# Clustered attention and two feed-forward blocks: float32 transposes and centroid products set behind single score and value products

## The chip, the cores and the metric

The kernel runs on one core of a Trainium2 chip. The metric is the device time of one execution in microseconds (us). Below, TensorE is PE in the rows (PEld are its weight loads), VectorE is DVE, ScalarE is ACT, GpSimd is POOL and SyncE, which issues the transfers, is SP.

## What is computed

For 2 batches of 8 heads, 768 tokens and 64 columns: attention in which a query sees only the keys of its own cluster, then two feed-forward blocks on the 1536 x 512 result.

```python
q_assign = argmax(q_n @ c_n.T)          # nearest of 16 centroids of the head, by cosine
k_assign = argmax(k_n @ c_n.T)
scores = where(q_assign == k_assign, q @ k.T / 8, -1e9)
attn = exp(scores - max); attn = attn / (sum(attn) + 1e-9)
x = (attn @ v) as [1536, 512]
x = softplus(x @ w_in) @ w_out                       # 512 -> 2048 -> 512
out = (silu(x @ w_gate) * (x @ w_val)) @ w_out2      # 512 -> 1536 -> 512
```

All of it is float32.

## The kernel before

A float32 number is split into two float32r parts, hi and lo, and a product is the sum of hi*hi, hi*lo and lo*hi. The attention goes over eight pairs of heads, twelve tiles of 128 queries to a pair, 96 tiles in all. The line numbers are those of the kernel before.

**A tile.** `sc` (L460) forms the scores of 128 queries against 768 keys, four products of 384 columns into a bank pair `sps`, and VectorE takes the negative row maximum `nm` (L474). One tile later, `ex` (L477) has ScalarE write exp of them to `p`. Two tiles later, `tr` (L488) transposes `p` on TensorE, six float32 transposes of 128 x 128 into two banks `tps`, three to a bank; each bank is emptied twice, by ScalarE as `th` (the hi part, L504) and by VectorE as `tl` (the lo part, L505). There are two such banks, so the first transpose of a tile needs the first `tl` of the tile before. `pv` (L507) adds six value products of 256 columns to `ops`, and every second tile ScalarE copies the sum to `xa`.

**A pair's preparation**, during the tiles of the pair before: `prep_x` (L332) transposes its queries and keys, four times three float32 transposes into the one bank `mps` of the pool `ps_m`, emptied by ScalarE to `xr`; `prep_split_rows` has GpSimd split `xr` and SyncE move the rows to the operands QT and KT; `prep_sims` (L385) forms the centroid products `sims`, twelve calls of 32 columns in float32 (each shows as two matmuls in the trace); `prep_arg` (L395) finds the one-hot of the largest in four steps, on VectorE but for a product with `wi` on GpSimd (L412); `prep_oht` (L425) transposes the one-hots `oh`, twice three float32r transposes, emptied by ScalarE to `OH`.

**A pair's end**, during the next pair: `rec` and `rec_rows` (L550, L557) bring the reciprocal row sums, by one transpose and two transfers through memory, to `R`; `fin` (L570) multiplies by it on GpSimd (`xu`), takes the hi part `XH` on ScalarE (L577) and the lo part `XL` on GpSimd.

**The order** is written by hand. `step(i)` emits, for tile i, scores, exp of i-1, transposes of i-2, then whatever the table of events has for the tile, then value products ("setvp", L683). The events are set by offsets from the pair's start (L652). Each engine runs its instructions in this order. The centroid products alone are spread: `between` holds them, and `tr` emits one behind each of its transposes. `pump(2)` after tiles 0 and 26 puts in the narrowing and splitting of a weight tile (five instructions on VectorE, L116 to L135).

Of the kernel before, what the change touches and what calls it, by code (L numbers as in the profile page):

```python
# [40 lines left out]
def kernel(  # L41
# [60 lines left out]
    def w_narrow(loaded):  # L102
        """float64 bits [p, a, f, 2] (low word, high word) -> float32 [p, a, f], in two steps

        For 2^-126 <= |x| < 2^128 the float32 exponent is the top bit and the low
        seven bits of the eleven; magnitudes below and above are brought to that
        range's ends first."""
# [37 lines left out]
    # units of the two feed-forward blocks; a unit's own tiles are split three units  # L145
    # ahead, the tile of the output product with the unit
# [14 lines left out]
    # the first tiles of the second block's values have room early on  # L161
# [23 lines left out]
    def split_tasks(batch):  # L185
        """two steps for each tile"""
# [21 lines left out]
    # work of the other engines that is emitted between parts of the products  # L208
    todo = collections.deque()

    def first_do(tasks):
        """before all others, but for the second step of a tile whose first was done"""
# [13 lines left out]
    # ================= attention =================  # L226
# [105 lines left out]
    def prep_x(pr, which, half):  # L332
        src = (qn_t, kn_t)[which][pr]
        if half == 0:
            xr_t[pr, which] = pre.tile([128, S], F32, tag=f"xr{which}", name="xr")
# [634 lines left out]
```

## Time and profile before

| | |
|---|---|
| median of 3 runs | 863.29 us (862.83 to 864.06) |
| span of the profiled execution, first to last instruction | 861.7 us |
| TensorE busy | 820.9 us, 95% |
| VectorE busy | 683.9 us, 79% |
| ScalarE busy | 397.6 us, 46% |
| GpSimd busy | 336.0 us, 39% |
| attention | to 266 us of the span, feed-forward blocks from there |

The profile gives one execution. Its own time is known by its span only; the median of the runs is 1.6 us above it. The busy shares are means over stages of different kinds: in the feed-forward blocks TensorE runs long products with the others far behind it, in the attention all four engines are near the end of their room, and what counts there is which of them a tile waits for.

### The profile page before, as it was taken

The page shows a single profiled execution, that of the slowest core. Times are in us where ns is not written, and L with a number is a line of the kernel's source. Part 1 is how long each engine was busy: PE and PEld are TensorE (multiplying, and loading weights), DVE is VectorE, ACT ScalarE, POOL GpSimd, SP SyncE. Part 2 cuts the span into 40 slices and gives each one's busy share as a digit, 9 for nine tenths or more (in the row PEclk, how much of TensorE's full clock was granted, in tenths as well). Part 3 has the DMA queues.
Part 4 walks back from the last instruction along what each step waited for, and adds up shares of the span by engine and source line. Part 5 has one row for each costly group of instructions (what it writes and reads, how often), then busy time and mean ns, then how long its engine had stood idle before and what let it go on. Part 6 is the DMA issues. An engine that isn't in the chain of part 4 may idle for free.

```text
span 861.7 us, 11737 instructions
## 1 busy us (share of the span) xinstructions
PE 820.9 (95%) x4366; PEld 697.5 (81%) x4366; DVE 683.9 (79%) x1016; ACT 397.6 (46%) x735; POOL 336.0 (39%) x229
## 2 busy tenths in 40 slices
PE   7999999999999999989898997799999999999998
PEld 6899999999898778768777786588888888888886
DVE  6888978988896778898888888849886868876464
ACT  4689889888893755433244433232212212120210
POOL 3636465555522545444244333424433312332110
PEclk9799999999999999999999999999999999999999
DMA  8975775575312132122221120202312221220003
GB/s 200 248 163 134 190 150 142 141 172 122 85 38 69 49 98 74 51 74 80 65 74 50 49 74 25 68 7 74 97 50 74 74 73 49 74 72 26 1 1 146
DMA packets 65336, 75.42 MB, mean 88 GB/s; under 512 B 28960, under 2 KB 51584, under 8 KB 65280
## 3 DMA queue, kind: packets, MB, share of 16 engines
q1 hardware_dynamic: 65280, 74.68, 32.3%
q8 instruction: 34, 0.56, 0.3%
q14 instruction: 22, 0.18, 0.1%
HBM read 48.27 MB, written 3.19 MB: 60 GB/s over the span
## 4 chain that ended last, share of the span: by engine, by line
PE 60%; DVE 25%; DMA 5%; issue 4%; ACT 4%; POOL 1%; SPq 0%; POOLq 0%; ACTq 0%; DVEq 0%
PE bank L731 28%; PE bank L913 11%; PE sps L466 5%; PE ops L515 5%; DVE m L116 5%; PE tps L498 5%; DVE acc L827 5%; DVE e L796 3%; PE bank L813 2%; DVE r L789 2%; DVE m L126 2%; DVE m L123 2%; DMA rd<-rt 2%; DMA R<-rd 2%; DVE whi L135 2%
## 5 line engine op out<-in xcount | busy, mean ns | idle before, releaser
L136 POOL TENSOR_TENSOR wlo<-m,whi 128x512 fp32r<-128x512 f32 x68 | 100.7, 1480 | 291.9 <-DVE whi L135 266.1
L116 DVE TENSOR_SCALAR m<-m 128x512 f32<-128x512 f32 x68 | 86.0, 1265 | 38.4 <-ACT m L115 38.4
L505 DVE TENSOR_TENSOR tl<-tps,th 128x384 fp32r<-128x384 f32 x192 | 98.8, 550 | 20.2 <-ACT th L504 19.6
L474 DVE TENSOR_REDUCE nm<-sps 128x1 f32<-128x768 f32 x96 | 91.3, 952 | 14.3 <-PE sps L466 11.4
L498 PE MATMUL tps<-id,p 128*128 128x128 f32 x576 | 95.3, 282 | 1.1 <-DVE tl L505 1.1
L504 ACT CAST th<-tps 128x384 fp32r<-128x384 f32 x192 | 84.6, 491 | 20.1 <-PE tps L498 17.1
L482 ACT ACTIVATE p<-sps,nm 128x768 f32<-128x768 f32 x96 | 88.1, 918 | 5.6 <-DVE nm L474 5.6
L466 PE MATMUL sps<-KT,QT 128*128 128x384 f32 x384 | 84.7, 343 | 5.6 <-ACT p L482 3.7
L731 PE MATMUL bank<-YH,whi 128*128 128x512 f32 x288 | 81.6, 391 | 2.5 <-DVE acc L827 2.5
L498 PEld LDWEIGHTS tps<-id,p 128*128 128x128 f32 x576 | 76.4, 153 | 8.4 <-DVE tl L505 5.1
L731 PE MATMUL bank<-YL,whi 128*128 128x512 f32 x288 | 81.6, 392 | 0.0
L731 PE MATMUL bank<-YH,wlo 128*128 128x512 f32 x288 | 81.6, 392 | 0.0
L769 ACT CAST gh<-e 128x1536 fp32r<-128x1536 f32 x16 | 23.7, 1481 | 122.8 <-DVE e L796 122.8
L515 PE MATMUL ops<-th,VV 128*128 128x256 f32 x288 | 79.7, 306 | 0.0
L813 PE MATMUL bank<-gh,whi 128*128 128x512 f32 x192 | 58.9, 407 | 17.3 <-DVE r L789 8.2
L115 ACT ACTIVATE m<-raw 128x512 f32<-128x512 f32 x68 | 44.5, 666 | 62.1 <-POOL wlo L136 62.0
L515 PE MATMUL ops<-tl,VV 128*128 128x256 f32 x288 | 71.9, 279 | 0.0
L770 POOL TENSOR_TENSOR gl<-e,gh 128x1536 fp32r<-128x1536 f32 x16 | 57.1, 3573 | 34.5 <-ACT gh L769 30.7
L466 PEld LDWEIGHTS sps<-KT,QT 128*128 128x128 f32 x384 | 63.4, 191 | 6.7 <-ACT p L482 4.4
L731 PEld LDWEIGHTS bank<-YH,whi 128*128 128x128 f32 x288 | 54.4, 189 | 14.3 <-issue 2.9
L731 PEld LDWEIGHTS bank<-YH,wlo 128*128 128x128 f32 x288 | 54.5, 189 | 11.4
L731 PEld LDWEIGHTS bank<-YL,whi 128*128 128x128 f32 x288 | 54.5, 189 | 11.3
(124 smaller groups left out, 1776.6 us busy)
## 6 DMA issues: line engine op xcount, KB each, us to landing
raw<-in_moe_w_out_dram SPq DMA_DIRECT2D x28, 512.0 KB, 3.3
raw<-in_moe_w_in_dram SPq DMA_DIRECT2D x16, 512.0 KB, 3.9
QT<-hi SPq DMA_DIRECT2D x32, 192.0 KB, 3.1
raw<-in_moe_w_val_dram SPq DMA_DIRECT2D x12, 512.0 KB, 4.0
raw<-in_moe_w_gate_dram SPq DMA_DIRECT2D x12, 512.0 KB, 3.5
KT<-hi SPq DMA_DIRECT2D x14, 384.0 KB, 5.8
qn<-in_q_dram SPq DMA_DIRECT2D x16, 192.0 KB, 5.7
kn<-in_k_dram SPq DMA_DIRECT2D x16, 192.0 KB, 4.2
```

What stands on the lines that cost most here:

```text
L116: nc.vector.tensor_scalar(out=m.bitcast(F32), in0=m.bitcast(F32), scalar1=F64_LEAST, scalar2=F64_MOST, op0=ALU.max, op1=ALU.min)
L136: nc.gpsimd.tensor_tensor(out=lo, in0=x, in1=_r(hi), op=ALU.subtract)
L466: nc.tensor.matmul(ps[:, c, 0:384], lhsT=Q[:, a, 128 * j:128 * j + 128], rhs=K[:, a, 384 * c:384 * c + 384], start=(a == 0), stop=(a == 1),)
L474: nc.vector.tensor_reduce(out=nm, in_=ps[:, :, 0:384], axis=AX.XY, op=ALU.max, negate=True)
L482: nc.scalar.activation(out=_h(p), in_=s_t.pop(i)[:, :, 0:384], func=AF.Exp, bias=nm_t.pop(i), accum_out=sm_t[pr][:, j:j + 1],)
L498: nc.tensor.transpose(ps[:, 128 * j:128 * j + 128], p[:, 128 * kb:128 * kb + 128], id32)
L504: nc.scalar.copy(th, pv)
L505: nc.vector.tensor_tensor(out=tl, in0=pv, in1=_r(th), op=ALU.subtract)
L515: nc.tensor.matmul(o[:, 0:CW], lhsT=VV_t[pr][:, hh, kb].rearrange("p a d -> p (a d)"), rhs=t[:, kb, :], start=(kb == 0 and lohi == 0), sto ...
L731: nc.tensor.matmul(banks[c], lhsT=wt[:, kk, :], rhs=xt[:, kk, 512 * c:512 * c + 512], start=(kk == 0 and wt is hi and xt is xh), stop=(kk ...
L813: nc.tensor.matmul(banks[NCH * d + c], lhsT=wt[:, 0, ds_], rhs=gt[:, 512 * c:512 * c + 512], start=(ff == 0 and n == 0), stop=(ff == 1 and ...
L913: nc.tensor.matmul(bk, lhsT=lhs[:, ts_], rhs=rhs[:, 0, :], start=(ff == 0 and n == 0), stop=(ff == 1 and n == 2),)
```

## The change

It touches the attention only. The transposes of a tile go to a queue `tq`, and a preparation's transposes, centroid products, one-hot transposes and the transpose of `rec_rows` to a queue `fill`. `slot` takes one item from them behind each single score product and each single value product: behind the first two scores only from `fill`, and there only items that open no new bank; behind the others from `tq` as long as it holds any, then from `fill`. One bank of `ps_m` may be opened in a tile. What is left of `tq` follows the value products. exp of the tile before is now emitted ahead of the scores, and the events behind all of these.

Four things change beside the order. A pair's preparation begins 17 tiles before the pair, not 14. The product with `wi` moves from GpSimd to VectorE, as a fifth step of `prep_arg`. The one-hots are float32, not float32r, so their transposes are too. `XH` of all pairs but the last is written by GpSimd, not ScalarE.

On TensorE, in a tile that carries centroid products of the next pair, there stands before (sps are scores, tps the transposes of p, sims the centroid products, ops the value products, each row a call):

```order
L466 MATMUL sps<-KT_101,QT_97 128x384 x4
L498 MATMUL tps<-id_67,p 128x128
L377 MATMUL sims<-C_176,xr 128x32
L498 MATMUL tps<-id_67,p 128x128
L377 MATMUL sims<-C_176,xr 128x32
```

and in such a tile now:

```order
L515 MATMUL sps<-KT_101,QT_97 128x384
L421 MATMUL sims<-C_176,xr 128x32
L515 MATMUL sps<-KT_101,QT_97 128x384
L421 MATMUL sims<-C_176,xr 128x32
L515 MATMUL sps<-KT_101,QT_97 128x384
L561 MATMUL tps<-id_67,p 128x128
L515 MATMUL sps<-KT_101,QT_97 128x384
L561 MATMUL tps<-id_67,p 128x128
L575 MATMUL ops<-th,VV 128x256
L561 MATMUL tps<-id_67,p 128x128
L575 MATMUL ops<-tl,VV 128x256
```

The first transpose of p now stands ahead of the fourth score, and a centroid product has products of the loop on both sides.

On VectorE, around the one-hots of a pair (mx, eq and oh are steps of them, rt the copy of `rec_rows`), there stands before:

```order
L401 TENSOR_REDUCE mx<-sims 128x24
L474 TENSOR_REDUCE nm<-sps 128x1
L505 TENSOR_TENSOR tl<-tps,th 128x3x128 x2
L407 TENSOR_TENSOR eq<-sims,mx 128x384
L474 TENSOR_REDUCE nm<-sps 128x1
L505 TENSOR_TENSOR tl<-tps,th 128x3x128 x2
L562 COPY rt<-mps 12x128
L474 TENSOR_REDUCE nm<-sps 128x1
L505 TENSOR_TENSOR tl<-tps,th 128x3x128 x2
L416 TENSOR_REDUCE mx_986<-eq 128x24
L474 TENSOR_REDUCE nm<-sps 128x1
```

and now:

```order
L442 TENSOR_REDUCE mx<-sims 128x24
L524 TENSOR_REDUCE nm<-sps 128x1
L546 TENSOR_TENSOR tl<-tps,th 128x3x128 x2
L448 TENSOR_TENSOR eq<-sims,mx 128x384
L524 TENSOR_REDUCE nm<-sps 128x1
L546 TENSOR_TENSOR tl<-tps,th 128x3x128 x2
L455 TENSOR_TENSOR eq<-eq,wi 128x384
L524 TENSOR_REDUCE nm<-sps 128x1
L546 TENSOR_TENSOR tl<-tps,th 128x3x128 x2
L623 COPY rt<-mps 12x128
L458 TENSOR_REDUCE mx_958<-eq 128x24
L465 TENSOR_TENSOR oh<-eq,mx_958 128x384
```

The step with wi has come in, and rt and the last two steps stand together between two tiles.

On ScalarE, where a new pair's first transposes are copied out (xr), there stands before:

```order
L504 CAST th<-tps 128x3x128 x2
L577 CAST XH<-xu 128x768
L343 ACTIVATE xr<-mps 128x384
L482 ACTIVATE p,sm<-sps,nm 128x768
L504 CAST th<-tps 128x3x128 x2
L343 ACTIVATE xr<-mps 128x384
```

and on GpSimd now, at the end of a pair:

```order
L639 TENSOR_TENSOR xu<-xu,R 128x768
L642 CAST XH<-xu 128x768
L646 TENSOR_TENSOR XL<-xu,XH 128x768
L394 CAST hi<-xr 128x768
L395 TENSOR_TENSOR lo<-xr,hi 128x768
```

XH has left the queue in which it stood ahead of xr, and stands on GpSimd between its neighbours.

The diff, cut to its core (dropped comments and moved lines are left out):

```diff
+    tq, fill = collections.deque(), collections.deque()
+    bank_left = [0]
+    def slot(early=False):
+        if tq and not early:
+            tq.popleft()()
+        elif fill:
+            opens, f = fill[0]
+            if opens and (early or not bank_left[0]):
+                return
+            bank_left[0] -= opens
+            fill.popleft()
+            f()
+    def opening(items):
+        return [(n == 0, f) for n, f in enumerate(items)]
...
+    def queue_x(pr, which, half):
+        fill.extend(opening(items_x(pr, which, half)))
+    def queue_sims(pr):
+        fill.extend(opening(items_sims(pr, 0) + items_sims(pr, 1)))
...
     def prep_arg(pr, step):
         if step == 0:
-            assert not between
+            while fill:
+                fill.popleft()[1]()
...
-            eng = nc.gpsimd if pr else nc.vector
-            eng.tensor_tensor(out=eq, in0=eq, in1=wi.unsqueeze(1).to_broadcast(full), op=ALU.mult)
+        elif step == 2:
+            nc.vector.tensor_tensor(out=eq, in0=eq, in1=wi.unsqueeze(1).to_broadcast(full), op=ALU.mult)
...
-                oh = oh_t[pr] = pre.tile(full, F32R, tag="oh", name="oh")
+                oh = oh_t[pr] = pre.tile(full, F32, tag="oh", name="oh")
...
     def sc(i):
         for a in range(2):
             for c in range(2):
                 nc.tensor.matmul(ps[:, c, 0:384], ...)
+                if (a, c) == (1, 1):
+                    nm = ...
+                slot(a == 0)
...
     def pv(c, part):
                 nc.tensor.matmul(o[:, 0:CW], ...)
+                slot()
...
         elif part == 1:
-            nc.scalar.copy(XH[:, m, cols], xu)
+            if eng is nc.gpsimd:
+                eng.tensor_copy(XH[:, m, cols], xu)
+            else:
+                nc.scalar.copy(XH[:, m, cols], xu)
...
-    REC = (1, 5, 8, 10, 11)
+    REC = (1, 4, 8, 9, 10)
...
-            o = L * pr - 14 if pr > 1 else 0
+                off = {'x': (0, 1, 2, 3), 's': 4, 'p0': 4, 'p1': 6, 'a': (7, 8, 9, 10, 10), 't': (10, 11), 'v': 10, 'lq': 4, 'lv': 13}
+                o = L * pr - 17
...
     def step(i):
+        bank_left[0] = 1
+        ex(i - 1)
+        queue_tr(i - 2)
+        sc(i)
+        pv(c, part)
+        while tq:
+            tq.popleft()()
+        for f, a in events.pop(i, []):
+            f(*a)
...
+    queue_sims(1)
     for i in range(N_IT + 1):
         step(i)
```

## Rows read from the trace of the kernel before

**Rows 1.** Busy time by stretch: us, then PE, PEld, DVE, ACT, POOL, PEclk, DMA, GB/s.

```profile
18.30:34.40 16.10, 13.19 (x68) 12.23 (x69) 11.83 (x18) 7.50 (x17) 8.93 (x8) 0.68 1.02 278
34.40:230.20 195.80, 192.18 (x1531) 182.96 (x1529) 168.12 (x285) 169.77 (x399) 105.08 (x85) 1.00 0.66 151
```

**Rows 2.** Timeline of a plain tile, all engines: start, us (merged), engine, line, operation.

```profile
236.82 0.86 PE L466 MATMUL sps<-KT,QT 128*128 128x384 f32 x4
...
237.52 0.82 PE L498 MATMUL tps<-id,p 128*128 128x128 f32 x6
...
237.72 0.96 DVE L474 TENSOR_REDUCE nm<-sps 128x1 f32<-128x768 f32 x1
...
238.60 1.01 DVE L505 TENSOR_TENSOR tl<-tps,th 128x384 fp32r<-128x384 f32 x2
...
238.88 0.51 PE L466 MATMUL sps<-KT,QT 128*128 128x384 f32 x2
```

**Rows 3.** Centroid products alone, ahead of the loop: ns min/median/max, first and last start.

```profile
L377 PE MATMUL sims<-C,xr x24: 195/276/277, 9.1 to 11.6; 128*128 128x32 f32 x24
```

**Rows 4.** Timeline of TensorE where the transpose of 12 columns follows the six.

```profile
63.98 0.82 PE L498 MATMUL tps<-id,p 128*128 128x128 f32 x6
64.63 0.28 PE L560 MATMUL mps<-id,r 128*12 128x128 f32 x1
```

**Rows 5.** Timeline of TensorE in a tile with centroid products between its transposes.

```profile
209.61 0.31 PE L498 MATMUL tps<-id,p 128*128 128x128 f32 x1
209.76 0.31 PE L377 MATMUL sims<-C,xr 128*128 128x32 f32 x2
209.90 0.31 PE L498 MATMUL tps<-id,p 128*128 128x128 f32 x1
```

**Rows 6.** Timeline of VectorE around a step of the one-hots.

```profile
217.97 1.02 DVE L505 TENSOR_TENSOR tl<-tps,th 128x384 fp32r<-128x384 f32 x2
218.91 0.54 DVE L416 TENSOR_REDUCE mx<-eq 128x24 f32<-128x384 f32 x1
219.37 0.95 DVE L474 TENSOR_REDUCE nm<-sps 128x1 f32<-128x768 f32 x1
```

**Rows 7.** Timeline of TensorE, the score products that begin a tile.

```profile
69.58 0.86 PE L466 MATMUL sps<-KT,QT 128*128 128x384 f32 x4
...
72.13 0.87 PE L466 MATMUL sps<-KT,QT 128*128 128x384 f32 x4
...
74.43 0.86 PE L466 MATMUL sps<-KT,QT 128*128 128x384 f32 x4
...
76.81 0.86 PE L466 MATMUL sps<-KT,QT 128*128 128x384 f32 x4
...
80.18 0.86 PE L466 MATMUL sps<-KT,QT 128*128 128x384 f32 x4
...
91.54 0.86 PE L466 MATMUL sps<-KT,QT 128*128 128x384 f32 x4
...
94.46 0.86 PE L466 MATMUL sps<-KT,QT 128*128 128x384 f32 x4
...
227.09 0.87 PE L466 MATMUL sps<-KT,QT 128*128 128x384 f32 x4
...
230.18 0.98 PE L466 MATMUL sps<-KT,QT 128*128 128x384 f32 x4 [0.87 <-ACT p L482]
```

**Rows 8.** Timeline of ScalarE and TensorE where XH stands ahead of xr.

```profile
77.81 0.83 ACT L577 CAST XH<-xu 128x768 fp32r<-128x768 f32 x1 [1.15 <-POOL xu L575]
...
79.09 0.55 PE L340 MATMUL mps<-id,qn 128*128 128x128 f32 x3 [0.76 <-ACT xr L343]
```

**Rows 9.** Timeline of VectorE with the weight tile, and with the copy rt.

```profile
88.72 0.43 DVE L116 TENSOR_SCALAR m<-m 128x512 f32<-128x512 f32 x1
...
91.44 0.95 DVE L474 TENSOR_REDUCE nm<-sps 128x1 f32<-128x768 f32 x1
...
97.75 0.27 DVE L562 COPY rt<-mps 12x128 f32<-12x128 f32 x1
```

More of the change, by code (lines that the diff above doesn't have):

```diff
@@ L330, in mbank, with do_all, items_x, item @@
         return pool.tile([128, 512], dt, tag=tag, name=name)
[L332 to L345 removed]
+    def do_all(items):
+        for item in items:
+            item()
+    def items_x(pr, which, half):
+        src = (qn_t, kn_t)[which][pr]
+        got = []
+        def item(j):
+            if j == 0:
+                if half == 0:
+                    xr_t[pr, which] = pre.tile([128, S], F32, tag=f"xr{which}", name="xr")
+                got.append(mbank())
+            ps, t = got[0], 3 * half + j
+            nc.tensor.transpose(ps[:, 128 * j:128 * j + 128], src[:, t].rearrange("p h d -> p (h d)"), id32)
+            if j == 2:
+                cols = slice(384 * half, 384 * half + 384)
+                xr = xr_t[pr, which]
+                if which == 0:
+                    nc.scalar.activation(out=xr[:, cols], in_=ps[:, 0:384], func=AF.Copy, scale=SCALE)
+                else:
+                    nc.scalar.copy(xr[:, cols], ps[:, 0:384])
+                x_done.add((pr, which, half))
+        return [functools.partial(item, j) for j in range(3)]
+    x_done = set()
+    def prep_x(pr, which, half):
+        do_all(items_x(pr, which, half))
+    def queue_x(pr, which, half):
+        fill.extend(opening(items_x(pr, which, half)))
     def prep_split(pr, which, eng, hilo=None):
+        assert {(pr, which, 0), (pr, which, 1)} <= x_done
         xr = xr_t[pr, which]
@@ L375, in sims_tile @@
     def sims_tile(pr, which, t):
+        if which == 0 and t == 0:
+            y_t[pr] = mbank(name="sims")
         y = y_t[pr]
@@ L383, in sims_tile, with items_sims @@
         )
-    def prep_sims(pr, which, spread=True):
-        if which == 0:
-            y_t[pr] = mbank(name="sims")
-        for t in range(NT):
-            if spread:
-                between.append(functools.partial(sims_tile, pr, which, t))
-            else:
-                sims_tile(pr, which, t)
+    def items_sims(pr, which):
+        return [functools.partial(sims_tile, pr, which, t) for t in range(NT)]
+    def queue_sims(pr):
+        fill.extend(opening(items_sims(pr, 0) + items_sims(pr, 1)))
     def prep_arg(pr, step):
@@ L486, in ex, with evac, queue_tr @@
         p_t[i] = p
-    def tr(i):
+    def evac(i, half, ps):
+        c, jj = divmod(i, CT)
+        th = th_t[c][:, 3 * half:3 * half + 3, 128 * jj:128 * jj + 128]
+        tl = tl_t[c][:, 3 * half:3 * half + 3, 128 * jj:128 * jj + 128]
+        pv = ps[:, 0:384].rearrange("p (a n) -> p a n", a=3)
+        nc.scalar.copy(th, pv)
+        nc.vector.tensor_tensor(out=tl, in0=pv, in1=_r(th), op=ALU.subtract)
+    def queue_tr(i):
         c, jj = divmod(i, CT)
@@ L493, in tr, with item @@
         p = p_t.pop(i)
-        for half in range(2):
-            ps = ps_t.tile([128, 512], F32, tag="t", name="tps")
-            for j in range(3):
-                kb = 3 * half + j
-                nc.tensor.transpose(ps[:, 128 * j:128 * j + 128], p[:, 128 * kb:128 * kb + 128], id32)
-                if between:
-                    between.popleft()()
-            th = th_t[c][:, 3 * half:3 * half + 3, 128 * jj:128 * jj + 128]
-            tl = tl_t[c][:, 3 * half:3 * half + 3, 128 * jj:128 * jj + 128]
-            pv = ps[:, 0:384].rearrange("p (a n) -> p a n", a=3)
-            nc.scalar.copy(th, pv)
-            nc.vector.tensor_tensor(out=tl, in0=pv, in1=_r(th), op=ALU.subtract)
+        banks = {}
+        def item(kb):
+            half, j = divmod(kb, 3)
+            if j == 0:
+                banks[half] = ps_t.tile([128, 512], F32, tag="t", name="tps")
+            ps = banks[half]
+            nc.tensor.transpose(ps[:, 128 * j:128 * j + 128], p[:, 128 * kb:128 * kb + 128], id32)
+            if j == 2:
+                evac(i, half, ps)
+        tq.extend(functools.partial(item, kb) for kb in range(NT))
     def pv(c, part):
@@ L568, in rec_rows, with queue_rec @@
         r_t[pr] = R
+    def queue_rec(pr):
+        fill.append((True, functools.partial(rec_rows, pr)))
     def fin(pr, part, eng, c0=0, c1=S):
@@ L615 @@
     mpool[0] = (ps_m, "m")
-    for n in range(4):
+    for n in range(5):
         prep_arg(0, n)
```

110 lines of the change are left out of this document (46 added, 64 removed).

## The prediction

> **What bounds the kernel now.** I read four views, in this order. The table by stretches says which engine fills the attention loop; the timeline of a plain tile says what a tile costs on each engine and who waits for whom; the rows of the other kinds of tile give the price of each extra; the starts of successive tiles show where TensorE waits. From 34.4 to 230.2 us TensorE is busy 192.2 of 195.8 us, VectorE 168.1, ScalarE 169.8, GpSimd 105.1 [rows 1]. So the loop is TensorE's, but not by much. A plain tile takes 2.06 us, from scores at 236.82 to scores at 238.88 [rows 2]: 0.70 for four score products, 0.65 for six transposes (the same six stand alone from 63.98 to 64.63 [rows 4]), 0.70 for six value products. VectorE works 1.82 of these: the row maximum nm holds it 0.88 (237.72 to 238.60 [rows 2]), the two subtractions tl 0.94 (217.97 to 218.91 [rows 6]). It is idle only 0.24 us in a plain tile. That nearness decides this forecast.
>
> The blocks behind 266.4 us are untouched, and I take their time as it is. The profiled span is 861.7 us and the median of the runs 863.29, 1.6 us more; the changes below are added to the median.
>
> **The change, step by step: what TensorE itself does.** The order of the 128x128 transposes is new, their number is not. A float32 transpose costs 0.11 us in a burst. Is that the load of its weights, which a longer product ahead could hide, or its own stream? In rows 4 the sixth transpose is followed by one with 12 weight columns only (mps<-id,r), and the six still take 0.65 us. A load of 12 columns cannot be what holds the sixth to 0.11, so it is the stream, and moving it behind a product gives nothing back. Nor does a change between the two kinds of product cost anything that I can see: 4 scores, 6 transposes and 6 value products fill the 2.06 us with two such changes, and no remainder over 0.01 us is left. The change makes ten more of them in a tile. The only excess I grant is that the weight load of the next product (0.11, below) just outlasts a transpose's stream: 0.002 us for five more in each of 94 tiles, **+1.0 us**, with -3 and +4 as bounds.
>
> The centroid products (sims) are another matter. Each is two short matmuls with a 128-column load each. Alone, 24 of them went out between 9.1 and 11.6 us [rows 3], 0.11 us each, far more than 32 columns can need: they run at the pace of their loads. Before, one call stood between two transposes: from 209.61 to 209.90 us, 0.29 for both [rows 5], so 0.18 for the call, since a transpose's own stream hides one load and the transpose's load is short (0.29 less two loads leaves 0.07). After, the call stands between two products of the loop. The product ahead hides its first load, but the second load and the load of the product behind lie open: 2 x 0.11 = 0.22. That is 0.04 dearer, for 12 calls in each of the six pairs prepared in the loop: 72 x 0.04 = **+2.9 us**. If loads could be drawn two ahead, the call would cost 0.14 and this term would be -2.9 instead; that is its other bound.
>
> The Trainium skill (TensorE: Matmul & The Clock Gate, LDWEIGHTS (loading the stationary operand)) puts a load at columns over 1.2, 107 ns for 128 columns, and lets it run under the matmul ahead. Rows 3 agree with it at 0.11. By that rule alone a call behind a product would take 0.214, the term would be +2.4 and the forecast 0.5 us lower; it speaks against this part of the change.
>
> The one-hot transposes (mps<-idr,oh) turn from float32r into float32. The second such tile took 74.43 - 72.13 = 2.30 us, 0.24 over plain for three [rows 7], 0.08 each; float32 ones cost 0.11. 42 x 0.03 = **+1.3 us**.
>
> **What goes away.** Before, the copy of XH stands in ScalarE's queue ahead of the copy that empties the bank of a new pair's first transposes. XH waited until 77.81 for GpSimd, and TensorE's next three transposes waited 0.76 for the bank, until 79.09 [rows 8]. That tile took 80.18 - 76.81 = 3.37 us against 2.39 for such a tile (2.06 and three transposes), and the last one of the kind, at 227.09, 3.09 against 2.06, its wait seen at 230.18 [rows 7]. Counted over five such places, with the tile behind each, 5.6 us. The change puts XH on GpSimd, whose queue has 195.8 - 105.1 = 90 us of room [rows 1], and starts the pair three tiles sooner, with an item or two behind each product: **-5.6 us** (or -4, if something else keeps the bank). The first one-hot tile took 2.55 against 2.30 for the second [rows 7]: TensorE waits there for the one-hots. After, the transposes stand at the end of the next tile: 6 x 0.25 = **-1.5 us**.
>
> **What comes new: VectorE.** This is the step I weigh most. Before, the first transpose of a tile stands 0.70 us behind the start of its scores (237.52 - 236.82), and nm starts at 0.90 (237.72) [rows 2]. The bank that this transpose fills is emptied by the first tl of the tile before, which ends at 0.90 + 0.88 + 0.55 = 2.33 (0.55 is the 1.02 of two in rows 6 less the 0.47 from one start to the next); it is wanted at 2.06 + 0.70 = 2.76. VectorE may run 0.43 us late. After, the transpose stands behind the third score, at 0.53, and itself puts the fourth score and so nm off by 0.11. The tl ends at 2.44 and is wanted at 2.59: 0.15 us of grace. One step of the one-hots holds VectorE 0.46 (218.91 to 219.37 [rows 6]), and before that was hidden but for 0.03: it stands there between tl and nm, which then starts late by as much [rows 6]. Now there are five steps, since the product with wi comes over from GpSimd; the first runs beside the last centroid products, four fall into tiles with almost nothing extra on TensorE, the last two into one, with the copy rt (0.27 [rows 9], 0.20 as the next begins before its end, which a one-hot step's 0.54 and 0.46 show too). Per pair: 4 x 0.46 + 0.20 = 2.04, less the grace 0.15, less two tiles' idle 0.48, less the four float32 transposes that TensorE does there, 0.44: 0.97 us in which TensorE waits. Six pairs: **+5.8 us**. The bounds are 0 (VectorE finds room) and 2.04 x 6 = 12.
>
> The weight tile that is split at tile 26 puts 2.72 us on VectorE (88.72 to 91.44 [rows 9]). Before, it stood between two long tiles, and cost the tile from 91.54 to 94.46 2.92 - 2.06 = 0.86 [rows 7], with the tile behind it 1.15. After, it stands behind the last centroid products and a one-hot step: the last of these products ends 0.28 us into the next tile (its length in rows 3), so nm can start at 0.28 + 0.46 + 2.72 = 3.46 instead of 1.01, 2.30 us late after the grace. 2.30 - 1.15: **+1.2 us**.
>
> **The start.** From 18.3 to 34.4 us the mean granted clock is 0.68 [rows 1], so TensorE has its lower level, 1.2 GHz, for some 10 of the 16 us (0.32 of the clock lost, at a half lost while it is low). The second pair's centroid products leave tiles 2 and 3 for tiles 0 to 2, where TensorE idled; it is fuller before the clock falls, which may shorten the slow stretch. Against that stand five one-hot steps in tiles 4 to 6, packed closer, 0.9 by the sum above, and 0.2 for a later first nm. I take **-0.6 us**: bounds -4 (no slow stretch, half of some 8 busy us) and +2.
>
> **The sum**: 1.0 + 2.9 + 1.3 - 5.6 - 1.5 + 5.8 + 1.2 - 0.6 = +4.5 us, 863.3 + 4.5 = **867.8 us**.
>
> **The rivals.** First, faster: VectorE never makes TensorE wait. Then the 5.8 is gone, and the weight tile costs nothing, not even its old 1.15: 867.8 - 5.8 - 1.2 - 1.2 = 859.6 us. For it: VectorE has 0.24 us idle in each tile [rows 2, 6] and took a one-hot step in its stride before. Against: that took a grace of 0.43, of which 0.15 is left. Second, no difference: half of these waits come, and the start gains 1 to 2 us, near 863.5. Third, much faster: a transpose behind a product costs 0.06 instead of 0.11, 0.05 x 6 x 94 = 28 us, near 840; rows 4 speak against it. Fourth, much slower: the first transpose is held by its semaphore so often that its load lies open too, 0.07 for each of some 500 places in an extreme, up to 35 us more; in plain tiles the grace is positive, so I give it little. The deciding point between the forecast and the first rival is whether tl of one tile ends 0.5 us behind the next tile's scores.
>
> **How the numbers follow.** Forecast, slower, 865 to 873: 0.51. First rival 0.22, third 0.03: faster 0.25. Second 0.22. Fourth 0.02 with the forecast: slower 0.53. The range takes in the first rival and the forecast with the larger half of the one-hot waits: 859 to 873; the 2 in 10 left out are the third and fourth and the outer ends of VectorE's term. A measurement of this kernel can tell about 0.2%, 1.7 us, from no change.
>
> **What would show it.** Right: a centroid call of 0.22 us; tiles of 2.06 us with transposes and products in turn; no wait of mps for xr; waits of tps for tl, 1 us in each pair, in the three tiles behind its last centroid products, and some 2 us at tile 27. Wrong: plain tiles shorter than 2.05 us (third rival), longer than 2.10 (the grace is already used up), or no waits for tl (first rival).

## The result and the profile after

| | before | after |
|---|---|---|
| median of four runs | 863.67 us (862.83 to 865.56) | 874.24 us (871.40 to 877.31) |
| span of the profiled execution | 861.7 us | 875.4 us |
| starts of the first score product, tile 12, tile 84, the last value product | 18.33, 50.11, 230.18, 266.04 us | 17.62, 52.72, 240.09, 277.30 us |

The ratio is 1.0123, with a 95% interval of 1.009 to 1.0156: slower by 1.2%, 10.6 us, where 4.5 us were forecast and 873 us was the upper end of the range. The direction was right, the size was not. The mean granted clock is not the cause: it was 0.982 to 0.990 (mean 0.986) in the four runs after and 0.986 on the mean over the 64 runs of the kernel before that stand beside it and the runs below. One of the four executions of the run burst2 below took 2087 us and is left out of its ratio.

By place, in the two profiled executions (tiles are counted from 0): 2.6 us were lost by tile 12, 7.3 in tiles 12 to 83 (187.4 against 180.1 us), 1.35 from tile 84 to the last value product, and 2.4 in the untouched blocks behind it, which had five stretches at the lower clock, of 3.4 us each, against three before. Such stretches come in another number in each execution (three to six in the traces below), so I take these 2.4 us as no part of the change.

The stretches of the kernel after, which answer to [rows 1] (the columns are those of [rows 1]; the third is the end of the attention):

```profile
17.60:33.70 16.10, 15.06 (x67) 14.00 (x68) 11.80 (x17) 7.36 (x16) 7.85 (x7) 0.58 1.00 272
33.70:240.10 206.40, 200.31 (x1533) 188.04 (x1532) 182.11 (x295) 171.09 (x395) 106.26 (x85) 1.00 0.63 144
240.10:277.40 37.30, 34.41 (x250) 31.78 (x249) 28.77 (x50) 27.31 (x63) 10.01 (x6) 1.00 0.13 36
```

TensorE is still 97% busy in the loop, now for 206.4 us instead of 195.8. The busy share doesn't show such a loss: in the centroid rows below the record of a score product lasts 0.42 us, though the next matmul starts 0.26 us behind it.

Two plain tiles, to set beside [rows 2] (start, us, engine, line, operation; the rows that the reading doesn't need are left out):

```profile
248.65 0.68 PE L515 MATMUL sps<-KT,QT 128*128 128x384 f32 x3
248.98 0.38 ACT L593 COPY xa<-ops 128x256 f32<-128x256 f32 x1
249.25 0.92 ACT L533 ACTIVATE p<-sps,nm 128x768 f32<-128x768 f32 x1
249.66 0.96 DVE L524 TENSOR_REDUCE nm<-sps 128x1 f32<-128x768 f32 x1
250.14 1.05 ACT L545 CAST th<-tps 128x384 fp32r<-128x384 f32 x2
250.66 1.12 DVE L546 TENSOR_TENSOR tl<-tps,th 128x384 fp32r<-128x384 f32 x2
250.74 0.69 PE L515 MATMUL sps<-KT,QT 128*128 128x384 f32 x3
251.27 0.14 PEld L561 LDWEIGHTS tps<-id,p 128*128 128x128 f32 x1 [0.16 <-DVE tl L546]
251.82 0.96 DVE L524 TENSOR_REDUCE nm<-sps 128x1 f32<-128x768 f32 x1
...
253.00 0.70 PE L515 MATMUL sps<-KT,QT 128*128 128x384 f32 x3
```

The tile from 248.65 to 250.74 took 2.09 us, the one behind it 2.26. (That one carries the transpose of 12 columns too; its like without it take 2.16.) In the second the first transpose waits for tl. But VectorE is hardly late: nm began at 249.66, and tl can follow it after 0.88 (as in [rows 2]), at 250.54. It begins at 250.66, since its th came only at 250.14, behind exp, which stands behind xa on ScalarE. In every second tile ScalarE has xa to copy, and there its chain takes most of the time. So the prediction's sign "longer than 2.10, the grace is already used up" came true, in half of the tiles and by an engine that it had not reckoned with.

A centroid call between two score products of the kernel after:

```profile
181.64 0.42 PE L515 MATMUL sps<-KT,QT 128*128 128x384 f32 x1
181.90 0.30 PE L421 MATMUL sims<-C,xr 128*128 128x32 f32 x2
182.03 0.42 PE L515 MATMUL sps<-KT,QT 128*128 128x384 f32 x1
```

From score to score it is 0.39 us; less the 0.175 of a score product alone, a call costs 0.22, as forecast.

To count the rest, I take each tile's length less what it carries, at the prices that the tiles without a wait and the spacing of starts give: before, 2.06 us for a plain tile and 0.11, 0.185 and 0.06 for a transpose of the preparation, a centroid call and a one-hot transpose; after, 2.084 and 0.1135, 0.2235 and 0.1125. (The 0.18 of [rows 5] is a call with a transpose behind it; the last of the six in a tile has a value product behind it, so a tile with six took 3.17, 0.185 a call.) What is left is called the wait of a tile below.

| tiles 12 to 83 | forecast, us | measured, us |
|---|---|---|
| order of transposes and products (72 x 0.025) | +0.8 | +1.8 |
| centroid calls (72 x 0.0385) | +2.9 | +2.8 |
| one-hot transposes and the wait for the one-hots | -0.4 | +1.9 |
| waits for xr gone (these tiles alone) | -5.1 | -5.1 |
| VectorE's waits | +5.8 | +4.2 |
| weight tile | +1.2 | +1.25 |
| five preparation transposes fewer in the stretch | | -0.3 |
| rests of 0.08 to 0.12 in nine tiles | | +0.8 |
| sum | +5.2 | +7.3 |

The worst line is the one-hots'. Their transposes, set a tile later so as not to wait, waited in all six pairs: 0.20, 0.20, 0.65, 0.43, 0.34 and 0.28 us, against 0.29 to 0.32 before. This is the wait in the start, at pair 1 (tile 6), where it was longest (VectorE, GpSimd and TensorE rows):

```profile
37.41 0.54 DVE L458 TENSOR_REDUCE mx<-eq 128x24 f32<-128x384 f32 x1
37.99 1.87 DVE L465 TENSOR_TENSOR oh<-eq,mx 128x384 f32<-128x384 f32 x1
39.79 0.94 DVE L524 TENSOR_REDUCE nm<-sps 128x1 f32<-128x768 f32 x1
...
37.63 1.82 POOL L395 TENSOR_TENSOR lo<-xr,hi 128x768 fp32r<-128x768 f32 x1 [0.21 <-DMA QT<-lo]
...
39.92 0.30 PE L477 MATMUL mps<-id,oh 128*64 128x128 f32 x1 [1.16 <-DVE oh L465]
```

The step oh takes 0.56 us elsewhere. Here it takes 1.87, and ends at 39.86, 0.41 us behind the end of GpSimd's lo at 39.45. In the seven pairs of this trace it took 0.56, 0.56, 0.63, 0.70, 0.78, 0.99 and 1.87 us, and each long one ended 0.41 to 0.42 us behind the end of a GpSimd instruction that was running when it began. That gave the theory for the second half of the experiments.

The theories at the start: **A**, the sum was right in kind, and the order on TensorE costs what it takes from VectorE's room; **B**, VectorE's extra work must be made good in whatever order.

### The profile page after: what moved, and what is told of

Its sections match the earlier page's. It is cut to its first block, busy times and chain, and to the rows that moved or that the text cites. A ratio compares the mean times of both kernels' runs of the same rounds, so it can differ in the third digit from the quotient of the medians.

```text
span 875.4 us, 11741 instructions
## 1 busy us (share of the span) xinstructions
PE 833.6 (95%) x4366; PEld 705.8 (81%) x4366; DVE 698.5 (80%) x1023; ACT 398.6 (46%) x728; POOL 336.2 (38%) x229
## 4 chain that ended last, share of the span: by engine, by line
PE 62%; DVE 29%; issue 4%; ACT 3%; DMA 1%; POOL 1%; SPq 0%; DVEq 0%; ACTq 0%
PE bank L793 27%; PE bank L975 11%; PE ops L575 6%; PE sps L515 6%; PE tps L561 6%; DVE m L116 5%; DVE acc L889 4%; PE bank L875 3%; DVE tl L546 3%; DVE nm L524 3%; DVE e L858 3%; DVE m L126 2%; DVE r L851 2%; DVE m L123 2%; DVE whi L135 1%
## 5 line engine op out<-in xcount | busy, mean ns | idle before, releaser
L561 PE MATMUL tps<-id,p 128*128 128x128 f32 x576 | 142.9, 278 | 3.8 <-DVE tl L546 3.4
L515 PE MATMUL sps<-KT,QT 128*128 128x384 f32 x384 | 117.4, 397 | 2.4 <-DMA KT<-khl 1.8
L546 DVE TENSOR_TENSOR tl<-tps,th 128x384 fp32r<-128x384 f32 x192 | 102.5, 553 | 11.0 <-ACT th L545 5.2
L545 ACT CAST th<-tps 128x384 fp32r<-128x384 f32 x192 | 91.5, 482 | 34.8 <-PE tps L561 32.8
L575 PE MATMUL ops<-th,VV 128*128 128x256 f32 x288 | 104.4, 363 | 1.4 <-DVE xu L597 1.4
L575 PE MATMUL ops<-tl,VV 128*128 128x256 f32 x288 | 102.1, 355 | 0.0
L561 PEld LDWEIGHTS tps<-id,p 128*128 128x128 f32 x576 | 81.1, 141 | 12.4 <-DVE tl L546 11.5
L515 PEld LDWEIGHTS sps<-KT,QT 128*128 128x128 f32 x384 | 69.6, 199 | 5.8 <-DVE KT L697 1.5
```

The costliest lines, as they stand in the source:

```text
L515: nc.tensor.matmul(ps[:, c, 0:384], lhsT=Q[:, a, 128 * j:128 * j + 128], rhs=K[:, a, 384 * c:384 * c + 384], start=(a == 0), stop=(a == 1),)
L545: nc.scalar.copy(th, pv)
L546: nc.vector.tensor_tensor(out=tl, in0=pv, in1=_r(th), op=ALU.subtract)
L561: nc.tensor.transpose(ps[:, 128 * j:128 * j + 128], p[:, 128 * kb:128 * kb + 128], id32)
L575: nc.tensor.matmul(o[:, 0:CW], lhsT=VV_t[pr][:, hh, kb].rearrange("p a d -> p (a d)"), rhs=t[:, kb, :], start=(kb == 0 and lohi == 0), sto ...
```

## The experiments

**XH alone.** The kernel before with the one edit that was to help:

```diff
-            nc.scalar.copy(XH[:, m, cols], xu)
+            if eng is nc.gpsimd:
+                eng.tensor_copy(XH[:, m, cols], xu)
+            else:
+                nc.scalar.copy(XH[:, m, cols], xu)
```

> The kernel before with one part of the change alone: XH of all pairs but the last is written by GpSimd, and nothing else moves. Theory (the term of -5.6 us in the prediction): the bank of a new pair's first transposes then comes free in time, the five waits of mps for xr (0.37 to 1.1 us in tiles 23, 35, 47, 71 and 83) and the 0.25 us behind each go away, and the last value product comes at 266.0 - 5.6 = 260.4 us, the median at about 858 us. Rival: the copy to xr is late for another reason (exp and the two th stand ahead of it too), XL comes later on GpSimd and holds something else: less than 2 us are gained, 862 to 864 us.

860.05 us, 0.9942 of the kernel before (0.9916 to 0.9968). Tiles 12 to 83 took 174.98 us, 5.1 less. Score products that begin a tile, ScalarE and GpSimd there, to set beside [rows 7] and [rows 8]:

```profile
77.17 0.86 PE L466 MATMUL sps<-KT,QT 128*128 128x384 f32 x4
78.53 0.49 PE L340 MATMUL mps<-id,qn 128*128 128x128 f32 x3
79.56 0.86 PE L466 MATMUL sps<-KT,QT 128*128 128x384 f32 x4
...
76.92 0.50 ACT L343 ACTIVATE xr<-mps 128x384 f32<-128x384 f32 x1
...
77.91 0.83 POOL L578 CAST XH<-xu 128x768 fp32r<-128x768 f32 x1
```

The tile that took 3.37 us takes 2.39. The prediction's largest gain is right, and it needs nothing of the new order: this version beats both kernels, the one before by 0.6%.

**The burst again.** First in a simple form, in which the places that the transposes left went to the other items:

```diff
-        if tq and not early:
-            tq.popleft()()
-        elif fill:
+        if fill:
...
             sc(i)
+        while tq:
+            tq.popleft()()
```

> The changed kernel with one part undone: the six transposes of a tile stand in one burst between its scores and its value products again; centroid products, the preparation's transposes and the rest stay behind single products. Theory A (the order on TensorE costs little by itself, but takes away VectorE's room): 0.025 us a tile come back (2.4 us), and with the first transpose back at 0.70 us behind the tile's start the waits of tps for tl, about 1.0 us in a pair, fall to some 0.3: 2.4 + 4 + 1 at the last tile = 7 us less, the last value product near 270 us instead of 277.3, median near 867. Theory B (VectorE's extra work has to be made good in any order): only the 2.4 us come back, last value product near 275 us, median near 872.

881.63 us, 1.0215 (1.019 to 1.0241), slower than the kernel after. It tells nothing of the burst: the one-hot transposes had moved up as well and waited 1.75 us a pair for the one-hots (10.5 us in six waits of mps for oh). So again, every other item held at its place:

```diff
-        if tq and not early:
-            tq.popleft()()
+        if skip[0] and not early:
+            skip[0] -= 1
...
+        skip[0] = len(tq)
             sc(i)
+        while tq:
+            tq.popleft()()
```

> The changed kernel with the six transposes of a tile in one burst between scores and value products, and every other item at exactly the place that it has in the changed kernel (in the run burst the one-hot transposes had moved up as well, and waited 1.75 us a pair for the one-hots). Theory A (the order takes away VectorE's room): 0.025 us a tile come back (2.4 us), tiles 84 to 94 are 2.06 us, and the waits of tps for tl in the one-hot tiles (about 0.33 + 0.38 us a pair) fall below 0.2 a pair; with 1 us at the last tile some 6 us less, last value product near 271 us with a start like that of the changed kernel. Theory B (VectorE's extra work has to be made good in any order): these waits stay, last value product near 274 us.

869.52 us, 1.0072 (1.0051 to 1.0094), 4.7 less than the kernel after. Tiles 84 to 94 are 2.06 us again but for two, and the end from tile 84 takes 35.3 us instead of 37.2; tiles 12 to 83 take 185.6 instead of 187.4. The wait of 0.33 us two tiles behind the last centroid products is gone (0.00). So the order took this room, as A says. The 0.38 in the tile behind VectorE's double step stays (0.35), as B says: there VectorE is later than any grace. And the wait for the one-hots grew from 2.1 to 3.9 us in six pairs, since oh was held longer (up to 1.68 us), which hides a part of the gain.

**One place later.**

```diff
-                slot(a == 0)
+                slot((a, c) != (1, 1))
```

> The changed kernel with the first transpose of a tile behind the fourth score, not the third; all six stand one product later, the preparation's items have one place less in a tile. Theory A (grace): the first transpose is wanted at 0.70 us and nm is not put off by it, so VectorE has about 0.43 us of grace again, not 0.15: the odd plain tiles of 2.16 us fall to 2.08, the waits for tl in the one-hot tiles to below 0.3 us a pair, 3 to 4 us less in all. Theory B (ScalarE's chain of xa, exp and th, or VectorE's sum of work, sets these tiles): they stay as they are, within 1 us.

874.81 us, 1.0135 (1.011 to 1.0161): no gain. The odd plain tiles fall to 2.08 us, as A says, and the even ones rise from 2.08 to 2.3. There the first value product waits for xa, since th and xa come later by a place. One such tile (ScalarE, then TensorE): xa ends at 251.83, and the value product starts at 251.88.

```profile
251.45 0.38 ACT L593 COPY xa<-ops 128x256 f32<-128x256 f32 x1
...
251.88 0.39 PE L575 MATMUL ops<-th,VV 128*128 128x256 f32 x1
```

Transposes among the value products need th late, and before the next value products ScalarE must still copy xa. With one bank for the sum, neither of the two places tried for the first transpose fits both.

**Centroid calls behind a transpose.**

```diff
         if tq and not early:
             tq.popleft()()
+            if fill and getattr(fill[0][1], "func", None) is sims_tile and (not fill[0][0] or bank_left[0]):
+                opens, f = fill.popleft()
+                bank_left[0] -= opens
+                f()
+        elif early and fill and getattr(fill[0][1], "func", None) is sims_tile:
+            return
```

> The changed kernel with the centroid products of the pairs 2 to 7 set behind a transpose (product, transpose, centroid product, product) and not between two products; all else as in it. Theory A (the term of the prediction: a transpose's stream hides one load of a call, a product ahead leaves two open): a call costs 0.18 instead of 0.22 us, 72 x 0.045 = 3.2 us less, last value product near 274 us, less what comes back where VectorE sets the pace. Rival: the load of the product behind the call lies open in either place, and a call costs 0.22 us: no difference.

886.95 us, 1.0269 (1.0248 to 1.0291). Of the 9.9 us more in tiles 12 to 83, 7.3 are my edit's: the first call now stands so close behind the last xr that it waits for it, and its tile is 1.15 to 1.46 us longer in each of the six pairs; 2.0 more stand behind the weight tile. The row of these waits (from 40 to 262 us: engine, line, waited for: us in total, times, longest), then a stretch of TensorE:

```profile
PE sims L427 <- ACT xr L381: 5.7, 6, 1.2
```

```profile
125.09 0.36 PE L581 MATMUL ops<-th,VV 128*128 128x256 f32 x1
125.29 0.27 PE L567 MATMUL tps<-id,p 128*128 128x128 f32 x1
125.40 0.31 PE L427 MATMUL sims<-C,xr 128*128 128x32 f32 x2
125.54 0.37 PE L581 MATMUL ops<-tl,VV 128*128 128x256 f32 x1
```

But the call's price can be read: product, transpose and call take 0.45 us; less 0.1175 and 0.11 that leaves 0.22. The rival is right. A transpose ahead hides nothing more than a product does; before, a call cost 0.18 [rows 5] because a transpose stood *behind* it. (That it is the transpose's shorter weight load that makes the difference is argued: no run parts it.)

**The last one-hot step and its transposes one tile later.**

```diff
-'a': (7, 8, 9, 10, 10), 't': (10, 11)
+'a': (7, 8, 9, 10, 11), 't': (11, 12)
```

> The changed kernel with the last one-hot step put one tile later, so that no tile has two steps and the copy rt, and the one-hot transposes one tile later. Theory A: the wait of the one-hot transposes for oh (0.2 to 0.65 us a pair) goes, and of the wait of tps for tl behind the double step (0.38 us a pair) most: 0.6 us a pair, 3 to 4 us in all, last value product near 274 us. Theory B: the late nm of the double step only moves to the next tile, since VectorE lacks room in every tile of this stretch: the waits for tl stay at 0.9 us a pair and only the wait for oh goes, 2 us less, near 275 us.

872.57 us, 1.0107 (1.0085 to 1.013). The wait for oh falls to 0.07 us, that behind the double step from 0.38 to 0.27, as A says: tiles 36 to 47 took 30.67 us, against 31.29. But in the pair behind that oh itself took 1.60 us beside GpSimd, and 0.8 and 0.4 us of waits came back behind it, and the weight tile's waits rose from 2.4 to 3.8 us, partly at the lower clock. The 3 to 4 us of A did not come: the interval overlaps that of the kernel after.

**The weight tile sooner**: behind tile 23, not 26 (`i in (0, 23)`).

> The changed kernel with its weight tile put in behind tile 23 instead of 26, ahead of the long tiles with centroid products. Theory A (a long VectorE step costs what the tiles behind it leave no room for): the 2.2 us of tile 28 and 0.2 of tile 29 fall to about 1 us in tiles 25 and 26, 1.3 us less. Theory B: the work is long against the grace anywhere, the wait only moves, within 0.3 us. Its start is that of the changed kernel, instruction by instruction: if the half-clock stretch of 13.65 us is a consequence of that order it comes again, if it varies between executions the first 12 tiles take 32 to 33 us instead of 35.1.

875.93 us, 1.0145 (1.0116 to 1.0173). The wait did not shrink, it came to 4.5 us in tile 25 and 2.2 in tile 26, partly at the lower clock. One step with two inputs in SBUF (L123, 0.69 us elsewhere) took 2.19 us beside GpSimd's lo. The stretch of 13.65 us at the lower clock came again in the start, where the first 12 tiles took 33.6 us.

**What holds VectorE.** Three runs bear on this. The kernel before with XH on GpSimd, and the product with wi on VectorE (the edit of XH and the new offsets of the steps are left out):

```diff
-            eng = nc.gpsimd if pr else nc.vector
-            eng.tensor_tensor(out=eq, in0=eq, in1=wi..., op=ALU.mult)
+        elif step == 2:
+            nc.vector.tensor_tensor(out=eq, in0=eq, in1=wi..., op=ALU.mult)
```

> The kernel before with XH on GpSimd, and the product with wi moved to VectorE as a fifth step in a tile of its own, as the change does; the order on TensorE stays. Theory A (with transposes in a burst VectorE has a grace of 0.43 us against a step of 0.46, as the prediction says): the step costs 0.1 us a pair or less, and the tiles 12 to 83 take 175.0 us as with XH on GpSimd alone, at most 0.6 more. Theory B (each step costs TensorE 0.46 less an idle of 0.24, whatever the order): 0.2 us a pair or more, 1.4 us in the six pairs.

862.63 us, 0.9993 (0.9979 to 1.0006): 2.6 us worse than with XH alone; tiles 12 to 83 took 179.8 us, 4.8 more. My theory A was wrong by its own sum: the step is the third in as many tiles. Where GpSimd was idle it cost 0.4 us a pair. Where not, up to 1.5 (VectorE, GpSimd, and TensorE behind it):

```profile
155.66 1.66 DVE L414 TENSOR_TENSOR eq<-eq,wi 128x384 f32<-128x384 f32 x1
...
155.06 1.84 POOL L549 TENSOR_TENSOR xu<-xu,xa 64x768 f32<-64x768 f32 x1 [1.53 <-DMA xu<-xa]
...
158.70 1.01 PE L499 MATMUL tps<-id,p 128*128 128x128 f32 x6 [1.16 <-DVE tl L506]
```

In the six pairs the step took 0.54, 0.54, 0.82, 0.88, 0.97 and 1.66 us, and the tile behind it waited 0.39, 0.39, 0.67, 0.73, 0.82 and 1.51: the step's length less 0.15, each time.

To part them, GpSimd's work was moved away from oh in the changed kernel:

```diff
-'t': (10, 11), 'v': 10, 'lq': 4, 'lv': 13}
+'t': (10, 11), 'v': 12, 'lq': 4, 'lv': 13}
...
-off = {'p0': 4, 'p1': 9,
+off = {'p0': 6, 'p1': 9,
...
-at(L * pr + (12, 17)[hh], merge, pr, hh)
+at(L * pr + (12, 18)[hh], merge, pr, hh)
```

> The changed kernel with three kinds of GpSimd work moved away from the last one-hot step: VV two tiles later, the merge of a pair's second head one tile later, the first split of pair 1 two tiles later. No instruction of VectorE or TensorE moves. In the changed kernel that step (oh from eq and mx) took 0.56 us where GpSimd was idle and 0.63 to 1.87 where it was at work, ending each time 0.40 us behind the end of a GpSimd instruction. Theory A (a VectorE instruction with two inputs in SBUF waits until GpSimd's running instruction is over): it takes 0.56 us in all pairs, the wait of the one-hot transposes falls to 0.2 us in each pair (from 0.20 to 0.65, and 1.46 at tile 6), 2 us less in all. Theory B (the step is long for another reason, such as its float32 output, or late inputs): the durations stay scattered, no difference.

876.44 us, 1.0133 (1.0105 to 1.016). For pair 1 it worked: oh took 0.60 us, and tile 6 waited 0.29 instead of 1.46. For the others it did not: GpSimd runs ahead of the tiles, and its next work stood beside oh as before. So in a second try a transfer keeps GpSimd waiting (VV at 13, and p0 of pair 1 at 6):

```diff
-at(L * pr + (10, 15)[hh], shift, pr, hh)
-at(L * pr + (12, 17)[hh], merge, pr, hh)
+at(L * pr + (10, 17)[hh], shift, pr, hh)
+at(L * pr + (12, 19)[hh], merge, pr, hh)
```

> The changed kernel with GpSimd kept idle beside the last one-hot step by what it waits for: the transfer that the merge of a pair's second head needs is issued two tiles later and the merge follows it, VV stands behind the merge, and the first split of pair 1 stands two tiles later (in the run port GpSimd ran ahead of its place and stood beside the step as before, but for pair 1). Theory A (a VectorE instruction with two inputs in SBUF is held until GpSimd's running instruction is over): the step oh takes 0.56 us in all pairs, the wait of the one-hot transposes 0.20 to 0.22 us in each, against up to 0.65 in the changed kernel, and tile 6 about 0.3 instead of 1.46: 0.9 and 1.2 us less. Theory B: durations of 0.6 to 1.0 us stay without GpSimd beside them.

881.97 us, 1.023 (1.0205 to 1.0254). The step oh took 0.56 us in all seven pairs, with GpSimd idle beside it, as A says. But GpSimd's lo had moved beside another step with two inputs in SBUF, the one with wi (VectorE, GpSimd, TensorE):

```profile
193.72 2.17 DVE L455 TENSOR_TENSOR eq<-eq,wi 128x384 f32<-128x384 f32 x1
195.81 0.94 DVE L524 TENSOR_REDUCE nm<-sps 128x1 f32<-128x768 f32 x1
...
198.37 0.56 DVE L465 TENSOR_TENSOR oh<-eq,mx 128x384 f32<-128x384 f32 x1
...
193.63 1.84 POOL L395 TENSOR_TENSOR lo<-xr,hi 128x768 fp32r<-128x768 f32 x1
...
197.27 0.33 PE L561 MATMUL tps<-id,p 128*128 128x128 f32 x1 [1.45 <-DVE tl L546]
```

This step had taken 0.55 us in each pair of the kernel after; now it took 2.22, 1.72 and 2.17 in three, and their tiles waited 1.9, 1.4 and 1.8 us. The hold goes where GpSimd goes: shown in both directions. (Another 3.0 us were lost from tile 84 on; what held them stays open.)

The Trainium skill (SBUF — State Buffer, SBUF: two separate sides) says that VectorE and GpSimd share one pair of ports, which a VectorE operation with two SBUF inputs takes as a lock against a GpSimd operation that reads SBUF, and that the later one is blocked for the other's whole instruction. These traces agree: the held step ends 0.40 to 0.42 us after the GpSimd instruction, whatever their overlap. In the kernel after, the steps that read one operand from PSUM (tl, eq from sims) and the reductions mx kept their 0.53 to 0.56 us beside GpSimd.

**The fifth step back to GpSimd**, in the changed kernel:

```diff
-            nc.vector.tensor_tensor(out=eq, in0=eq, in1=wi..., op=ALU.mult)
+            eng = nc.gpsimd if pr else nc.vector
+            eng.tensor_tensor(out=eq, in0=eq, in1=wi..., op=ALU.mult)
```

> The changed kernel with the product with wi on GpSimd again, its place in the order unchanged. Theory A (the prediction's sum: steps in successive tiles add up, less 0.24 us idle a tile and the grace once): VectorE has one step of 0.46 us less in the three successive tiles, the wait for tl of 0.33 us two tiles behind the last centroid products goes, about 2 us in six pairs. Theory B (the product takes 1.0 us on GpSimd and stands behind GpSimd's other work, so VectorE's next step waits for it and holds nm): as much is lost as won, within 1 us, or slower.

873.67 us, 1.0121 (1.0103 to 1.0138): no difference from the kernel after. The waits of 0.33, 0.20 and 0.38 us stay at 0.32, 0.19 and 0.38, and the five pairs without a weight tile take 154.2 us instead of 154.5. So the fifth step, unheld, cost nothing there, and the prediction's four steps in a row were counted too evenly: the waits for tl come behind the first two steps and behind the double one.

**Towards a better kernel.** From XH alone, the one-hot transposes a tile later (`'t0': 11, 't1': 12`); then the weight tile's two steps apart (behind tiles 25 and 26); then also the first weight tile behind tiles 13 and 14 instead of 0; last, the weight steps apart with the one-hots at their old place:

> The kernel before with XH on GpSimd and the one-hot transposes one tile later; VectorE's steps and the order on TensorE stay. Theory A (in the first one-hot tile TensorE waits for the one-hots themselves): the 0.30 us of tiles 20, 32, 44, 56, 68 and 80 go, and only these, 1.8 us less than with XH alone, about 858 us. Theory B (this wait is for VectorE being late with tl, the one-hots only stand beside it): it stays, and nothing is gained.

> As the run xh_t, and the two steps of the weight tile stand one behind tile 25 and one behind tile 26, not both behind 26. Theory A (a VectorE step costs nothing where the tile behind it is long enough: tiles 26 and 27 carry centroid products and have 3.17 us for VectorE's 1.8): the waits of 0.87 us in tile 28 and 0.29 in tile 29 go, and no other comes: 1.1 us less than xh_t. Theory B (the steps hold VectorE in any tile): the wait only moves to tiles 26 and 27.

> As the run xh_t_w, and the first weight tile, behind tile 0 until now, in its two steps behind tiles 13 and 14. In the start TensorE waits 1.35 and 1.48 us in tiles 2 and 3 for p, whose row maximum stands behind this tile's 3.6 us on VectorE. Theory A: these two waits go, 2 to 2.8 us less than xh_t_w at tile 12, and tiles 14 to 16 stay as they are. Theory B (the granted clock decides the start; a fuller TensorE is slowed more): the first 12 tiles stay at 31 to 33 us.

> The kernel before with XH on GpSimd, and the two steps of its weight tile one behind tile 25 and one behind tile 26; the one-hot transposes at their old place (in the runs xh_t they shared the one bank with the next pair's first transposes and waited 1.34 us a pair). Theory A: the wait in tile 28 falls from 0.87 to 0.19 us as in xh_t_w, all else is as with XH alone: 0.7 us less, some 859.5 us, 0.5 per cent below the kernel before. Theory B: no difference from XH alone.

867.98, 868.21, 866.31 and 860.95 us, ratios 1.0042 (1.0021 to 1.0064), 1.0039 (1.0022 to 1.0056), 1.0017 (0.9998 to 1.0036) and 0.9967 (0.9952 to 0.9982). The first three share my mistake: the second half's transposes now stand in one tile with the next pair's first ones, and there is one bank for both (waits in the first of them):

```profile
PE mps L340 <- ACT OH L433: 5.6, 5, 1.1
```

And the 0.30 us that were to go became 0.15 and 0.25 in two tiles: that wait was VectorE's (B). The weight steps apart took the wait of 0.87 us in tile 28 to 0.19 (A), and in the last run to 0.32, but there one transfer of one-hots came late (score products of tile 36):

```profile
110.23 0.95 PE L466 MATMUL sps<-KT,QT 128*128 128x384 f32 x4 [0.99 <-DMA KT<-OH]
```

so nothing was gained over XH alone, whose interval overlaps. Whether the first weight tile is better behind tile 13 stays open: the clock was low for 17 us around that start, against 6.8 to 10.2 in the others of this order but one, which had no such stretch there.

## Why the forecast was short

Without the 2.4 us of the untouched blocks, the profiled pair lost 11.3 us. Split as the prediction's terms fall, 2.9 us of what was not forecast lie in the start, 2.1 in tiles 12 to 83 and 1.7 from tile 84 on.

**Right.** The gain from XH (5.1 of the 5.1 us due in these tiles, and shown alone); the weight tile (1.25 for 1.2, at tile 28, one later than foretold); the centroid call (0.2235 for 0.22); VectorE as the engine that TensorE waits for in the one-hot tiles, 4.2 us where 5.8 were forecast. That the size is near is in part luck, as the waits do not come by the steps as counted. The rivals "VectorE never makes TensorE wait" and "a transpose behind a product costs 0.06" are refuted by the waits for tl and by the 0.11 of every transpose, and the rival of an open load at some 500 places by plain tiles of 2.08 us.

**Failed: "wait for the one-hots gone, -1.5".** The step read the 0.25 us of the first one-hot tile as a wait for the one-hots; when their transposes alone were moved (run xh_t), 0.15 and 0.25 us of waits for VectorE's tl stayed in two tiles. It assumed that a tile's delay is enough and gave the steps on VectorE a fixed 0.46 us. In the double step's tile oh is ready too late even unheld (0.20 us a pair), and GpSimd held it in four of six pairs: 0.45 + 0.23 + 0.14 + 0.08 = 0.9 us more, and 1.26 more at tile 6, in the start. The old place of the step had GpSimd idle beside it in all six pairs of the loop's steady part (0.55 us each). That an engine with 90 us of room can still stop another was not among the prediction's resources. The float32 transposes themselves, forecast at 0.03 us more each, cost 0.05 more.

**Failed: "the start, -0.6".** Tile 12 came 2.6 us later. 1.3 of it is the held step at tile 6. The clock adds at most some 1.7, an estimate: TensorE ran at its lower level, 1.2 GHz, for 13.65 us of the start, against 10.24 before, and half of the difference is lost. But this differs between executions with the same order on TensorE in the start (17.60 to 33.70 us, runs spread and port, to be set beside the first row of the kernel after):

```profile
17.60:33.70 16.10, 14.53 (x79) 13.03 (x80) 14.05 (x22) 9.14 (x20) 7.82 (x7) 0.79 1.00 272
```

```profile
17.60:33.70 16.10, 15.70 (x61) 14.37 (x62) 11.30 (x17) 6.50 (x14) 7.19 (x7) 0.51 1.07 277
```

Whether the new order makes a long stretch likelier is open: the lower level held for 6.8 to 17.1 us, 12.3 on the mean, in the ten traces with the new start and its variants, and for 0 to 10.2, 8.0 on the mean, in six with the old one. The two overlap.

**Mis-sized: the order, +1.0.** Each place costs 0.0035 us with a value product and 0.005 with a score, not 0.002: 0.025 a tile, 2.4 us over 96. The odd plain tiles add 0.06 to 0.15 each, some 0.5 us in all, by ScalarE's chain, which the prediction did not look at. And the end cost 1.1 us that no step counted. The last tile has no scores, so a value product now stands ahead of its first transpose, and waits for the one bank of the sum (kernel after):

```profile
267.23 0.39 PE L575 MATMUL ops<-th,VV 128*128 128x256 f32 x1 [1.39 <-DVE xu L597]
```

From the scores of the last tile to the last value product it is 13.77 us, against 12.63 before and 12.51 with the burst (burst2).

**Left open.** How much of the start's 2.6 us belongs to the change, since its clock differs so between executions; the 0.38 us behind the double step, which the run spread took to 0.27 and no run to nothing; and the float32 one-hots and the earlier start of a pair, which no run undid alone.

## What to carry to other kernels

Before work is moved on or to VectorE, list which of its instructions read two operands from SBUF and what GpSimd does in the same microsecond: here such an instruction lasted until a GpSimd instruction that was already running was over, and GpSimd, which runs ahead of the order, must be kept away by what it waits for, not by its place in the program. Count each engine's chain through a tile, also of the one that is not the bottleneck: here ScalarE's copy, exp and copy set every second tile once the transposes were spread. And try the parts of a bundle alone: moving XH was worth all of the gain that was found.

## What the runs showed of the hardware

- A VectorE instruction of 0.55 us with two SBUF inputs took 0.6 to 2.2 us where a GpSimd instruction was already running, with its end 0.40 to 0.42 us after GpSimd's. A small one with a single input, sm (128x12, 0.16 us), took up to 1.77 us too beside lo (kernel after), with its end 0.03 us after lo's.
- A centroid call of two short float32 matmuls costs 0.18 us with a transpose behind it ([rows 5]) and 0.22 with a product behind it, whether a product (kernel after) or a transpose (run sims_behind) stands ahead.
- Behind the wait of 2.1 to 4.5 us that the weight tile causes, TensorE's granted clock fell to its lower level for 3.4 or 6.8 us in five of the ten traces that have this wait, and stayed at its higher level in five, the kernel after among them.
